# Issuing 24 DRAM stores of an FFT-and-FFN backward kernel from ScalarE's queue instead of SyncE's

## The chip, the cores and the metric

The kernel runs on one core of one Trainium2 chip. The metric is the device time of one execution in microseconds (us). Eleven executions of the kernel before had a median of 735.56 us (729.26 to 739.6). One further execution was profiled; it took 735.9 us, of which the profile covers a span of 734.2 us.

## The reference

The function computes a block with a gated state-space convolution and returns the output with the gradients of all parameters (outputs 0 to 11). Cut to what matters:

```python
xn = layernorm(x)                                     # x: 2048 x 512
K  = einsum(C, exp(dt*A*l), dt*B).real                # one filter of length 2048 for each of 512 channels
y  = irfft(rfft(pad(xn)) * rfft(pad(K)))[:L] + xn*Dskip
o  = silu(xn @ w1) @ w2                               # w1: 512 x 1792, w2: 1792 x 512
out = x + y * silu(o)
grads = vjp(out)(grad_out)    # d x, d A, d B, d C, d log_dt, d Dskip, d w1, d w2
```

## The kernel before

Everything is bf16 with sums in PSUM. The 512 channels are four blocks `b` of 128; the 2048 positions are 16 tiles of 128. The Fourier transforms are matmuls in two steps with a DMA transpose between them.

- **Forward, about 20 to 267 us.** `gen_tables` makes the exponentials of block `b` on VectorE and ScalarE and the filter out of them (matmuls L447 and L458), and stores it to `Kd` (L482, from ScalarE's queue). `gen_conv_x` transforms block `b` of `xn` with `dft_fwd` (matmuls L286, transposes L288, matmuls L297 and L298) and stores the spectrum `U` to `Ud` (L497). `gen_conv_fwd` transforms the filter, loads `U` back (L488), stores the filter's spectrum `KX` to `KXd` (L511), multiplies the two and transforms back (`dft_inv`, matmuls L310 and L319). These generators are woven block by block. `gen_ffn_fwd` (matmuls L541 and L558) is paced against them and fills TensorE.
- **Gates, about 265 to 305 us.** `gen_gate_rows` makes `do`, the gradient of `o`, and `ds`, the gradient of `y`, on ScalarE, VectorE and GpSimd.
- **Backward of the convolution, about 315 to 468 us.** `gen_conv_bwd` transforms `ds`, loads `Ud` and `KXd` (L488), multiplies, transforms back and stores `dKd` (L657, from ScalarE's queue) and `dUd` (L667). `gen_ffn_da` is paced against it: matmuls L886 into `ps_da`, VectorE's product L888, store `DHd` (L891), then for each 128 rows the matmuls L897 into `ps_dx`, ScalarE's copy of it to the tile `pd_s`, and the store of `pd_s` to `Pd` (L900). `pd_s` has one buffer, so that its next copy waits until the store has landed. `gen_out` makes output 0 (loads L614, L616, L618).
- **Gradients of the state-space parameters and of the weights, about 468 us to the end.** `gen_ssm_bwd` (loads L680 and L711, transposes L718, matmuls L729, L751 and L755), the rest of `gen_ffn_da` until 543 us, `gen_dw2` (L929), `gen_ln_bwd` (which loads `Pd` at L964), and last, from 671 us, `gen_dw1` (L947) alone on TensorE.

`k.evc` and `k.evb` are helpers of class `Evac` with the pattern "A": their copies out of PSUM run on ScalarE and all stand at L44 in the profile. So `U`, `KX` and `pd_s` are all written by ScalarE.

The order of the instructions on each engine isn't that of the source alone. The generators give priorities, and a scheduler orders the instructions when the program is built, with its own estimate of when each one could run; it inserts all waits too. Each engine then runs its list in order, and an instruction that waits holds all behind it on that engine. [...] SyncE computes nothing here: it issues DMAs, 24 of them the stores of this change.

Of the kernel before, what the change touches and what calls it, by code (L numbers as in the profile page):

```python
# [121 lines left out]
def turned_rows(k, pool, src, c, name, ev):  # L122

    out = pool.tile([P, 8, P], BF16, name=name, tag=name, bufs=2)
    turned(k, lambda i: src[:, 2 * c + i // 4, i % 4 * P:i % 4 * P + P], 8, out, ev)
    return out
# [149 lines left out]
def dft_fwd(k, w8, U, ev):  # L276

    nc, pc = k.nc, k.pc
    A = w8.tile([P, 2, 16, P], BF16, name="dA", tag="w8")
    Av = A[:].rearrange("p c g (t e) -> p c g t e", e=8)  # L280
    B = w8.tile([P, 2, 16, P], BF16, name="dB", tag="w8")
    for c in range(2):
        for h in range(2):
            ps = pc.tile([P, 8, P], F32, name="ps_s1", tag="pc")
            for j in range(8):
                nc.tensor.matmul(out=ps[:, j], lhsT=k.TF[:, 8 * h + j, c, :], rhs=U(8 * h + j), start=True, stop=True)  # L286
            ev(Av[:, c, :, 8 * h:8 * h + 8, :], ps[:].rearrange("p t (g e) -> p g t e", e=8))
        nc.sync.dma_start_transpose(B[:, c], A[:, c].rearrange("p g k -> p (g k)"))  # L288
    for _ in range(LAG):
        yield  # L290
    F2 = k.F2
    for h in range(2):
        for c, (m0, m1) in enumerate(((0, 1), (2, 0))):
            ps = pc.tile([P, 8, P], F32, name="ps_s2", tag="pc")
            for u in range(2):
                g0 = 8 * h + 4 * u
                nc.tensor.matmul(out=ps[:, 4 * u:4 * u + 4], lhsT=F2[:, m0], rhs=B[:, 0, g0:g0 + 4, :], start=True, stop=False)  # L297
                nc.tensor.matmul(out=ps[:, 4 * u:4 * u + 4], lhsT=F2[:, m1], rhs=B[:, 1, g0:g0 + 4, :], start=False, stop=True)  # L298
            ev(A[:, c, 8 * h:8 * h + 8, :], ps[:])
    return A, B  # L300


def dft_inv(k, A2, Y, ev, consume):

    nc, pc = k.nc, k.pc
    for g0 in range(0, 16, 4):
        ps = pc.tile([P, 4, 32, 8], F32, name="ps_i2", tag="pc")
        for g in range(4):
            for c in range(2):
                nc.tensor.matmul(out=ps[:, g], lhsT=Y[:, c, g0 + g, :], rhs=k.I2[:, c].rearrange("p c m -> p (c m)"),  # L310
                                 start=(c == 0), stop=(c == 1))
        ev(A2[:].rearrange("p c t (g e) -> p g (c t) e", e=8)[:, g0:g0 + 4], ps[:])
    yield
    for h in range(2):
        ps = pc.tile([P, 8, P], F32, name="ps_i1", tag="pc")
        for j in range(8):
            t = 8 * h + j
            for c in range(2):
                nc.tensor.matmul(out=ps[:, j], lhsT=k.TI[:, 2 * t + c, :], rhs=A2[:, c, t, :], start=(c == 0), stop=(c == 1))  # L319
        consume(8 * h, 8, ps)  # L320


def cplx_mul(k, w8, a, b, conj=False):

    TT = k.nc.vector.tensor_tensor
    n = 8
    for g0 in range(0, 16, n):
        gs = slice(g0, g0 + n)
        t2 = w8.tile([P, 2, n, P], BF16, name="cm2", tag="cm2")
        TT(out=t2[:, 0], in0=b[:, 1, gs], in1=a[:, 1, gs], op=ALU.mult)  # L330
        TT(out=t2[:, 1], in0=b[:, 0, gs], in1=a[:, 1, gs], op=ALU.mult)
        TT(out=b[:, :, gs], in0=b[:, :, gs], in1=a[:, 0:1, gs].to_broadcast([P, 2, n, P]), op=ALU.mult)  # L332
        TT(out=b[:, 0, gs], in0=b[:, 0, gs], in1=t2[:, 0], op=ALU.add if conj else ALU.subtract)  # L333
        if conj:
            TT(out=b[:, 1, gs], in0=t2[:, 1], in1=b[:, 1, gs], op=ALU.subtract)
        else:
            TT(out=b[:, 1, gs], in0=b[:, 1, gs], in1=t2[:, 1], op=ALU.add)
# [148 lines left out]
def spectrum_in(k, w8, b, which):  # L486
    t = w8.tile([P, 2, 16, P], BF16, name="sp_in", tag="w8")
    k.nc.sync.dma_start(t[:].rearrange("p c g k -> p (c g k)"), {"U": k.Ud, "K": k.KXd}[which][b])  # L488
    return t


def gen_conv_x(k, b):

    bs = slice(b * P, b * P + P)
    dft = k.dft
    U, _ = yield from dft_fwd(k, dft, lambda t: k.xn[:, t, bs], k.evc)
    k.nc.sync.dma_start(k.Ud[b], U[:].rearrange("p c g k -> p (c g k)"))  # L497
    yield


def gen_conv_fwd(k, b):

    nc, dft = k.nc, k.dft
    bs = slice(b * P, b * P + P)
    Kb = dft.tile([P, 4, 16, 32], BF16, name="Kb", tag="t4")
    nc.sync.dma_start(Kb[:].rearrange("p a t q -> p a (t q)"), k.Kd[b].rearrange("a i (r s) x -> (i r) a (s x)", s=2))
    for _ in range(LAG):
        yield
    KX, A2 = yield from dft_fwd(k, dft, lambda t: Kb[:, :, t, :], k.evc)
    U = spectrum_in(k, dft, b, "U")  # L510
    nc.sync.dma_start(k.KXd[b], KX[:].rearrange("p c g k -> p (c g k)"))  # L511
    yield
    cplx_mul(k, dft, KX, U)
    S = dft.tile([P, 16, P], BF16, name="S_b", tag="t4")

    def consume(t0, n, ps):
        xd = dft.tile([P, 8, P], BF16, name="xd", tag="cm2")
        nc.vector.tensor_tensor(out=xd[:], in0=k.xn[:, t0:t0 + n, bs], in1=k.Dbc[:, bs].unsqueeze(1).to_broadcast([P, n, P]), op=ALU.mult)
        nc.vector.tensor_tensor(out=S[:, t0:t0 + n], in0=ps[:], in1=xd[:], op=ALU.add)
    yield from dft_inv(k, A2, U, k.evc, consume)  # L520
    k.S_b = S
    (nc.scalar if b == 3 else nc.sync).dma_start(k.Sd[b], S[:].rearrange("p t d -> p (t d)"))
    yield
# [336 lines left out]
def gen_ffn_da(k, da):  # L860
    nc = k.nc
    D, FT, DK, T = k.D, k.FT, k.DK, k.T
    for c in range(T // 2):
        if c == 0:
            dN = turned_rows(k, da, k.do, 0, "doT", k.evb)
        dT = dN
        dTv = dT[:].rearrange("p (t k) n -> p t k n", k=DK)
        dhs = []
        for f in range(FT // 2):
            if f in (0, 4):  # L870
                n = 8 if f == 0 else 6
                sl = da.tile([P, 8, 256], BF16, name="slope", tag="slope", bufs=2)
                dh = da.tile([P, 8, 256], BF16, name="dhT", tag="dhT", bufs=3)
                nc.sync.dma_start(sl[:, 0:n], k.Hd[2 * f:2 * f + n, :, 256 * c:256 * c + 256].rearrange("f p n -> p f n"))
                nc.scalar.activation(out=dh[:, 0:n], in_=sl[:, 0:n], func=ACT.Silu)
                nc.scalar.activation(out=sl[:, 0:n], in_=sl[:, 0:n], func=ACT.Tanh, scale=0.5)
                slope_less_one(nc, dh[:, 0:n], sl[:, 0:n])
                dhs.append(dh)
            if f == 4 and c + 1 < T // 2:
                dN = turned_rows(k, da, k.do, c + 1, "doT", k.evb)  # L880
            i0 = 2 * (f % 4)
            ps = k.pf.tile([P, 2, 256], F32, name="ps_da", tag="pf")
            for j in range(2):
                ft = 2 * f + j
                for dk in range(DK):
                    nc.tensor.matmul(out=ps[:, j], lhsT=k.W2[:, ft, dk * P:dk * P + P], rhs=dTv[:, :, dk, :],  # L886
                                     start=(dk == 0), stop=(dk == DK - 1))
            nc.vector.scalar_tensor_tensor(out=dh[:, i0:i0 + 2, :], in0=dh[:, i0:i0 + 2, :], scalar=1.0, in1=ps[:], op0=ALU.add, op1=ALU.mult)  # L888
            if f in (3, 6):
                f0, n = (0, 8) if f == 3 else (8, 6)  # L890
                nc.sync.dma_start(k.DHd[f0:f0 + n, :, 256 * c:256 * c + 256].rearrange("f p n -> p f n"), dh[:, 0:n])  # L891
            yield
        for t in range(2):
            pd = da.tile([P, D], BF16, name="pd_s", tag="pd_s", bufs=1)
            ps = k.pf.tile([P, D], F32, name="ps_dx", tag="pf")
            for ft in range(FT):
                nc.tensor.matmul(out=ps[:], lhsT=dhs[ft // 8][:, ft % 8, t * P:t * P + P], rhs=k.W1[:, :, ft * P:ft * P + P],  # L897
                                 start=(ft == 0), stop=(ft == FT - 1))
            k.evb(pd[:], ps[:])
            nc.sync.dma_start(k.Pd[:, 2 * c + t, :], pd[:])  # L900
            yield


# [81 lines left out]
def kernel(ctx, tc, A_u, A_A_re, A_A_im, A_B_re, A_B_im, A_C_re, A_C_im, A_log_dt, A_Dskip, B_x, B_w1, B_w2, grad_out,  # L985
# [125 lines left out]
    for i in range(4):  # L1111
        next(bwd)
    ffb = gen_ffn_da(k, da)
    paced(bwd, woven([ffb, out], [2, 1]), BR)
    es_x.close()
# [35 lines left out]
```

## Time and profile before

| | |
|---|---|
| median of 11 executions | 735.56 us |
| profiled execution, and its span | 735.9 us, 734.2 us |
| mean granted TensorE clock | 0.934 of full speed |
| TensorE busy | 602.2 us, 5500 matmuls |
| VectorE busy | 548.2 us |
| ScalarE busy | 507.1 us |
| GpSimd busy | 108.1 us |
| SyncE's DMA queue q1 | 135.29 MB, packets 69.8% of 16 engines' span |
| ScalarE's DMA queue q10 | 4.98 MB, 2.1% |

In a line on a group or a wait, L12 is line 12 of the kernel; `out<-in` gives the tiles. PE is TensorE, ACT ScalarE, DVE VectorE, POOL GpSimd, SP SyncE; with a q behind it, the name means the engine's sequencer (issuing a DMA or handling a semaphore) and not its arithmetic. Issuing a DMA isn't counted as busy time. "us to landing" is the time from a DMA's issue until its last byte is confirmed.

### The profile page before, as it was taken

How to read it: one execution, taken by the hardware profiler on the slowest of the kernel's cores; microseconds unless marked ns; L12 is line 12 of the kernel's file. 1: busy time of each engine (PE TensorE's matmuls, PEld its weight loads, DVE VectorE, ACT ScalarE, POOL GpSimd, SP SyncE). 2: the span in 40 equal slices, each digit the busy share in tenths (PEclk: the TensorE clock that was granted, in tenths of full speed). 3: DMA queues.
4: the chain of work that ended last, by engine and by line, in shares of the span. 5: the costliest groups of instructions: out<-in, count | busy, mean ns of one | idle time of the engine just before them, and what ended most of it. 6: DMA issues, size and time to landing. Idle time of an engine off the chain costs nothing.

```text
span 734.2 us, 14020 instructions
## 1 busy us (share of the span) xinstructions
PE 602.2 (82%) x5500; PEld 432.1 (59%) x5500; DVE 548.2 (75%) x1086; ACT 507.1 (69%) x707; POOL 108.1 (15%) x180
## 2 busy tenths in 40 slices
PE   0668969979999966577989889978799978889995
PEld 0435646565675643354757567657576655656784
DVE  6969996969988759878898789747796685896000
ACT  6777758779889866947979688636746867782211
POOL 2172100000010035700000000000002003113210
PEclk9777998989999996879999989999999989999998
DMA  9876847769679876589988954789989999831772
GB/s 284 314 175 191 268 169 198 274 169 288 270 195 281 323 265 162 168 197 282 315 194 269 239 171 170 180 189 220 223 168 256 276 253 264 227 131 56 154 185 60
DMA packets 207042, 159.26 MB, mean 217 GB/s; under 512 B 129024, under 2 KB 185344, under 8 KB 203392
## 3 DMA queue, kind: packets, MB, share of 16 engines
q1 hardware_dynamic: 193856, 135.29, 69.8%
q0 software_dynamic: 6224, 18.10, 7.0%
q10 hardware_dynamic: 6896, 4.98, 2.1%
q8 instruction: 43, 0.70, 0.4%
q14 instruction: 23, 0.19, 0.1%
HBM read 65.14 MB, written 62.26 MB: 174 GB/s over the span
## 4 chain that ended last, share of the span: by engine, by line
issue 52%; POOL 5%; DVE 5%; DMA 3%; PE 0%; ACT 0%; POOLq 0%; ACTq 0%; SPq 0%; DVEq 0%
DMA out_dram<-o 1%; POOL out_dram L932 1%; DMA out_dram<-gout 1%; DVE YD L599 1%; DMA Kd<-KE 1%; POOL out_dram L809 1%; POOL out_dram L624 1%; DVE ds L595 1%; DMA Gr<-in_grad_out_dram 1%; DVE sp_in L332 1%; POOL out_dram L951 1%; POOL out_dram L980 1%; POOL g L598 0%; DVE YD L603 0%; DVE YD L601 0%
## 5 line engine op out<-in xcount | busy, mean ns | idle before, releaser
L44 ACT CAST dA<-ps_s 128x1024 bf16<-128x1024 f32 x96 | 94.2, 1031 | 18.7 <-PE ps_s L298 10.2
L886 PE MATMUL ps_da<-doT,W 128*128 128x256 bf16 x448 | 61.9, 281 | 9.8 <-DVE dhT L888 5.8
L541 PE MATMUL ps_h<-XT,W 128*128 128x256 bf16 x448 | 63.6, 293 | 1.3 <-ACT hT L44 0.7
L310 PE MATMUL ps_i<-I,sp_in 128*128 128x256 bf16 x384 | 53.5, 283 | 8.8 <-DVE sp_in L333 4.2
L558 PE MATMUL ps_o<-W,aT 128*128 128x512 bf16 x224 | 57.1, 393 | 2.8 <-ACT aT L549 2.6
L739 DVE TENSOR_TENSOR Tp<-Vb,Eb 128x1344 bf16<-128x1344 bf16 x64 | 51.9, 851 | 6.7 <-issue 5.4
L886 PEld LDWEIGHTS <-W 128*128 128x128 bf16 x448 | 44.2, 101 | 19.8 <-issue 11.4
L897 PE MATMUL ps_dx<-W,dhT 128*128 128x512 bf16 x224 | 54.7, 384 | 0.5 <-ACT doT L44 0.5
L44 ACT CAST dB<-ps_i 128x1024 bf16<-128x1024 f32 x48 | 47.0, 1019 | 10.6 <-PE ps_i L310 8.2
L541 PEld LDWEIGHTS <-W 128*128 128x128 bf16 x448 | 46.2, 105 | 13.1 <-issue 2.7
L947 PE MATMUL ps_w<-dh_tok,xn 128*128 128x256 bf16 x448 | 50.4, 273 | 2.2 <-DMA dh_tok<-DHd 1.7
L929 PE MATMUL ps_w<-YD,a_tok 128*128 128x512 bf16 x224 | 52.1, 379 | 0.0
L44 ACT CAST o<-ps_w 128x256 bf16<-128x256 f32 (+1 forms) x42 | 18.6, 443 | 48.3 <-PE ps_w L947 41.3
L310 PEld LDWEIGHTS <-sp_in 128*128 128x128 bf16 x384 | 37.1, 101 | 23.7 <-DVE sp_in L333 8.2
L947 PEld LDWEIGHTS <-xn 128*128 128x128 bf16 x448 | 43.4, 98 | 8.3 <-issue 3.1
L44 ACT CAST Vb<-ps_v 128x672 bf16<-128x672 f32 x64 | 43.0, 731 | 6.2 <-PE ps_v L729 6.2
L888 DVE SCALAR_TENSOR_TENSOR dhT<-dhT,ps_da 128x512 bf16<-128x512 bf16 x56 | 37.4, 682 | 12.9 <-PE ps_da L886 12.3
L729 PE MATMUL ps_v<-Gb,YT 128*128 128x168 bf16 x256 | 28.8, 243 | 18.4 <-ACT Vb L44 14.8
L297 PE MATMUL ps_s<-dB,F 128*128 128x512 bf16 x96 | 38.5, 407 | 5.9 <-DMA dB<-dA 4.1
L286 PEld LDWEIGHTS <-TF 128*128 128x128 bf16 x384 | 27.4, 105 | 25.3 <-issue 14.6
L419 ACT ACTIVATE sn<-V 128x1024 bf16<-128x1024 int32 (+3 forms) x40 | 34.8, 886 | 8.3 <-DVE V L417 8.1
L298 PE MATMUL ps_s<-dB,F 128*128 128x512 bf16 x96 | 38.0, 401 | 1.9 <-DMA dB<-dA 1.9
(223 smaller groups left out, 1384.0 us busy)
## 6 DMA issues: line engine op xcount, KB each, us to landing
Yd<-YD SPq DMA_DIRECT2D x8, 1024.0 KB, 5.4
sp_in<-Ud SPq DMA_DIRECT2D x8, 1024.0 KB, 7.4
h_in<-Hd SPq DMA_DIRECT2D x14, 512.0 KB, 5.4
Ed<-E SPq DMA_DIRECT2D x8, 672.0 KB, 5.4
Eb<-Ed SPq DMA_DIRECT2D x8, 672.0 KB, 5.6
Hd<-hT POOLq DMA_DIRECT2D x8, 512.0 KB, 6.5
Ud<-dA SPq DMA_DIRECT2D x4, 1024.0 KB, 9.6
KXd<-dA SPq DMA_DIRECT2D x4, 1024.0 KB, 6.3
```

Of the source, the lines that this page charges most:

```text
L44: return self.nc.scalar.copy(out=out, in_=in_)
L297: nc.tensor.matmul(out=ps[:, 4 * u:4 * u + 4], lhsT=F2[:, m0], rhs=B[:, 0, g0:g0 + 4, :], start=True, stop=False)
L298: nc.tensor.matmul(out=ps[:, 4 * u:4 * u + 4], lhsT=F2[:, m1], rhs=B[:, 1, g0:g0 + 4, :], start=False, stop=True)
L310: nc.tensor.matmul(out=ps[:, g], lhsT=Y[:, c, g0 + g, :], rhs=k.I2[:, c].rearrange("p c m -> p (c m)"), start=(c == 0), stop=(c == 1))
L541: nc.tensor.matmul(out=ps[:, j], lhsT=k.W1[:, dk, ft * P:ft * P + P], rhs=XTv[:, :, dk, :], start=(dk == 0), stop=(dk == DK - 1))
L558: nc.tensor.matmul(out=ps[:], lhsT=aT[:, ft, t * P:t * P + P], rhs=k.W2[:, ft, :], start=(ft == 0), stop=(ft == FT - 1))
L739: k.nc.vector.tensor_tensor(out=Tp[:, c, :, r ^ c].rearrange("p e (q w) a -> p q w e a", w=2), in0=Vb[:, :, c].rearrange("p q w (e a) -> p ...
L886: nc.tensor.matmul(out=ps[:, j], lhsT=k.W2[:, ft, dk * P:dk * P + P], rhs=dTv[:, :, dk, :], start=(dk == 0), stop=(dk == DK - 1))
L888: nc.vector.scalar_tensor_tensor(out=dh[:, i0:i0 + 2, :], in0=dh[:, i0:i0 + 2, :], scalar=1.0, in1=ps[:], op0=ALU.add, op1=ALU.mult)
L897: nc.tensor.matmul(out=ps[:], lhsT=dhs[ft // 8][:, ft % 8, t * P:t * P + P], rhs=k.W1[:, :, ft * P:ft * P + P], start=(ft == 0), stop=(ft ...
L929: nc.tensor.matmul(out=ps[:], lhsT=at[:, t, :], rhs=k.do[:, t, :], start=(t == 0), stop=(t == k.T - 1))
L947: nc.tensor.matmul(out=ps[:], lhsT=k.xn[:, t, dk * P:dk * P + P], rhs=dh[:, t].rearrange("p j n -> p (j n)"), start=(t == 0), stop=(t == k ...
```

## The change

Three stores are issued from ScalarE's queue and no longer from SyncE's. Four stores of `U`, four of `KX` (1 MB each) and sixteen of `pd_s` (128 KB each) are concerned. Nothing else in the source is changed; the scheduler orders the whole program anew.

```diff
@@ gen_conv_x
     U, _ = yield from dft_fwd(k, dft, lambda t: k.xn[:, t, bs], k.evc)
-    k.nc.sync.dma_start(k.Ud[b], U[:].rearrange("p c g k -> p (c g k)"))
+    k.nc.scalar.dma_start(k.Ud[b], U[:].rearrange("p c g k -> p (c g k)"))
@@ gen_conv_fwd
     U = spectrum_in(k, dft, b, "U")
-    nc.sync.dma_start(k.KXd[b], KX[:].rearrange("p c g k -> p (c g k)"))
+    nc.scalar.dma_start(k.KXd[b], KX[:].rearrange("p c g k -> p (c g k)"))
@@ gen_ffn_da
             k.evb(pd[:], ps[:])
-            nc.sync.dma_start(k.Pd[:, 2 * c + t, :], pd[:])
+            nc.scalar.dma_start(k.Pd[:, 2 * c + t, :], pd[:])
```

## The prediction

> **What bounds the kernel now.** I read the page's busy times first, then sums by stretch, then the waits of ScalarE and of SyncE's queue, and last single instructions in time.
>
> ```profile
> PE 602.2 (82%) x5500; PEld 432.1 (59%) x5500; DVE 548.2 (75%) x1086; ACT 507.1 (69%) x707; POOL 108.1 (15%) x180
> ```
>
> No engine is full. The stretches of 75 us (bounds; busy us and instructions of PE, PEld, DVE, ACT, POOL; granted clock; DMA share; GB/s) show who sets the pace where the sixteen Pd stores lie:
>
> ```profile
> 375.00:450.00 75.00, 65.15 (x550) 46.86 (x549) 64.04 (x92) 57.27 (x63) 4.04 (x6) 0.95 0.80 227
> 450.00:525.00 75.00, 64.09 (x623) 48.71 (x623) 53.59 (x73) 47.64 (x56) 0.51 (x1) 0.95 0.88 193
> ```
>
> TensorE is at 85 to 87%, ScalarE at 64 to 76%. So TensorE sets the pace, with 10 to 11 us idle in 75, and ScalarE has 17 to 27 us spare. A stall of ScalarE costs time only where TensorE then runs out of inputs or PSUM. TensorE's own waits, summed over its whole list, are 50.0 us for ScalarE (44 waits) and 56.8 us for VectorE (30 waits). I let half of a ScalarE stall reach the end.
>
> What SyncE's queue waits for (total us, times, longest):
>
> ```profile
> SPq L900 <- ACT pd_s L44: 17.9, 7, 4.2
> SPq L511 <- ACT dA L44: 12.5, 3, 6.0
> SPq L497 <- ACT dA L44: 1.5, 2, 0.9
> ```
>
> In 31.9 us SyncE stands at one of the 24 stores until ScalarE has copied, and all loads behind it stand too. That is what the change takes out of SyncE's list. Is anybody late because of it? ScalarE's waits for DMAs:
>
> ```profile
> ACT go_g L621 <- DMA go_g<-Od: 12.8, 6, 5.0
> ACT pd_s L44 <- DMA Pd<-pd_s: 3.6, 1, 3.6
> ACT dhT L875 <- DMA slope<-Hd: 3.3, 4, 1.3
> ```
>
> The longest of the first group ends at 421.11. SyncE before it:
>
> ```profile
> 407.08 7.16 SPq L288 DMA_TRANSPOSE dB<-dA  x2
> 414.34 0.57 SPq L891 DMA_DIRECT2D DHd<-dhT  x1
> 415.00 0.55 SPq L900 DMA_DIRECT2D Pd<-pd_s  x1
> 415.64 0.41 SPq L616 DMA_DIRECT2D go_g<-Od  x1
> ```
>
> The load of go_g was held by 7.16 us of issuing transposes and by 0.55 us of Pd. Most of those 12.8 us stay, then. The 3.6 us are another matter: that pd_s copy (489.99) waited for a Pd store whose data were ready at 471.2 and which SyncE, busy with transposes, issued only at 487.64. From ScalarE's queue it goes at once.
>
> [...] So I expect nothing of bandwidth. The trace agrees as far as it goes: 512 KB of Sd landed in 2.6 us from ScalarE and in 3.0 us from SyncE. [...] the trace shows ScalarE idle for 2.38 us while four Kd stores are issued. [...] Then a store from ScalarE could stand behind a transpose that SyncE is issuing. The only pair of this kind in the trace is at the start:
>
> ```profile
> 1.26 0.45 ACTq L1039 DMA_DIRECT2D Dbc<-in_A_Dskip_dram  x1
> 1.26 1.24 SPq L346 DMA_TRANSPOSE par_Ar<-in_A_A_re_dram  x1
> ```
>
> ScalarE wasn't held there, with queues still empty. No row shows it with full ones.
>
> **The change part by part**, against the profiled execution of 735.9 us (span 734.2 us, 1.7 us around it).
>
> (a) Issuing. Removed from SyncE are 24 issues at a median of 0.32 to 0.37 us, 8.5 us; SyncE isn't the limit, so this by itself gives nothing. Added to ScalarE are 24. The nearest rows are its own:
>
> ```profile
> 352.15 0.57 ACT L44 CAST pd_s<-ps_dx 128x512 bf16<-128x512 f32 x1
> 352.27 0.42 ACTq L657 DMA_DIRECT2D dKd<-dK  x1
> 352.74 1.93 ACT L44 CAST dB<-ps_i 128x1024 bf16<-128x1024 f32 x2
> ```
>
> The store of dK (copied until 352.25) is issued while the next copy runs, and the copy after that starts 0.02 us behind it: one instruction between copy and store hides the issue. Without it ScalarE loses 0.37 us and about 0.1 us of overlap between neighbours. In the changed program's order, 8 of the 24 stores stand directly behind their copy (one KX, seven Pd); 13 have one instruction between, 3 more. Sum: 8 x 0.47 = 3.8 us of ScalarE, half of it on the path: **+1.9**. If the cover of the 16 others were gone too: 24 x 0.47 = 11.3 us of ScalarE.
>
> (b) New waits. Fifteen of the 24 stores also wait for an earlier DMA [...]. Behind each stand ScalarE's copies out of PSUM, and TensorE behind those. The closest case is the tenth Pd store, which waits for the par_Br transpose only 83 instructions earlier in the program; that one is issued behind two transposes of 1.3 us, while ScalarE has a 1.5 us activation, the next pd_s copy and another 1.5 us before it. I bound all fifteen by 0 below and by three stalls of 3 us above and take one of 2 us, half on the path: **+1**.
>
> (c) [...] SyncE issues 24 dB transposes at a median of 3.3 us (80 us of the 381 between 54 and 435 us, 21%) and YT and par transposes in about half of 468 to 550 us (median 1.7 us). At half a transpose per hit: 17 stores x 0.21 x 1.65 = 5.9, and 7 x 0.5 x 0.85 = 3.0; together 8.9 us of ScalarE. Below, 0, by the pair at 1.26. I take a third, 3 us, half on the path: **+1.5**.
>
> (d) SyncE's list runs freer. Above: all of the 12.8, 3.6 and 3.3 us that ScalarE waits for go_g, Pd and slope, halved, about 10. Below: 0. I take the 3.6 us whole, of which half counts, and little else: **-2**. Next late would be the transposes themselves, which stay on SyncE.
>
> (e) The order. TensorE's list has the same 5500 matmuls, but moved: in the backward convolution those of L310, L319 and L297 stand 3 to 12 us of matmul time earlier, those of L886 up to 19 us later, some of L541 up to 28 us later; the last part (L947 alone) is as before. Counting in the program the waits of TensorE on ScalarE or VectorE whose producer stands under 10 instructions earlier, I find 63 where there were 55. At TensorE's mean wait for ScalarE, 50.0 / 44 = 1.1 us, eight more cost up to 9 us; the same moves could as well close gaps, so -4 below. I take **+2.5**.
>
> Sum: 1.9 + 1 + 1.5 - 2 + 2.5 = +4.9, so 740.8 us as a profiled execution. The median of the runs shown is 0.3 us under it: **740.5 us**.
>
> **Rivals.**
> - No measurable change, 736 us. Issues are hidden, and the reordering evens out. For it: ScalarE's 17 to 27 us spare per stretch, 16 of 24 stores not directly behind their copies (there the change isn't even what its words say). Chance 0.22.
> - Faster, 728 us. The relief of SyncE's list decides: loads and transposes come earlier by part of the 31.9 us, and (d) gives 8 with nothing given back. It decides if go_g's 12.8 us fall under 5 us and (a) to (c) stay under 2 us. Against it: the long holds on SyncE are its own transposes. Chance 0.18.
> - Much slower, 751 us. [...] 8.9 (c) + 3.8 (a) + 3 (b) reach TensorE whole, 15.7, while (d) and (e) about cancel; less the 0.3 to the median. It decides once ScalarE's stores take over 1 us each at the median. Chance 0.15.
> - The forecast, +0.7%, its own range 737 to 746. Chance 0.45, of which 0.05 lies under the bound below.
>
> **How the numbers follow.** A measurement of this kernel can tell about 0.5% (3.7 us) from no change. Faster is the third case's 0.18; same is 0.22 + 0.05 = 0.27; slower 0.40 + 0.15 = 0.55. The range reaches into the faster case by (d) with little given back, 730, and over the much slower one, 753.
>
> **What would show it.** (a): ScalarE's DMA issues at L497, L511 and L900 near 0.37 us each, and few gaps behind them. (b): ScalarE's waits naming a DMA ahead of these lines. (c): such an issue of over 1 us while SyncE has a transpose. (d): no wait of pd_s for Pd; go_g still waited for. (e): TensorE's busy time unchanged, its idle time moved between stretches, the sum some 5 us larger. I would be wrong if the waits of go_g vanish and the span falls, or if ScalarE's busy share stays and TensorE's idle time grows by over 10 us.

## The result and the profile after

The changed kernel took 747.2 us at the median of 12 executions (742.75 to 753.68). The kernel before took 735.64 us beside it (47 executions). The ratio is 1.0166, 95% interval 1.0142 to 1.0189. The change costs 1.7%, or 12 us; the forecast was 740.5 us. Disturbed executions are left out of all comparisons. The profiled executions have spans of 744.8 and 734.2 us, both at a mean clock of 0.934.

The page of the changed kernel, busy times and DMA queues:

```profile
PE 603.7 (81%) x5500; PEld 432.8 (58%) x5500; DVE 548.9 (74%) x1086; ACT 507.3 (68%) x707; POOL 102.0 (14%) x180
...
q1 hardware_dynamic: 190400, 124.80, 63.7%
...
q10 hardware_dynamic: 10352, 15.47, 5.8%
```

The work is the same: no engine's busy time grows by more than 1.5 us, and GpSimd's falls by 6. The bytes of the 24 stores have moved from q1 to q10. So the time lies in waits. TensorE's waits, summed over its whole list, are 130.0 us where they were 120.4.

What the stores cost where they now stand. First all sixteen of Pd (duration in ns: minimum, median, maximum; then from issue to landing), then one store on ScalarE's list, then a store of the spectrum `U` and the transpose that SyncE was issuing at the time:

```profile
L900 ACTq DMA_DIRECT2D Pd<-pd_s x16: 326/327/457, 357.4 to 557.0; - x16
...
DMA to landing us min/median/max: 1.7/3.3/6.0
```

```profile
64.35 0.62 ACT L44 CAST hT<-ps_h 128x512 bf16<-128x512 f32 x1
64.51 0.34 ACTq L497 DMA_DIRECT2D Ud<-dA  x1
65.00 1.91 ACT L549 ACTIVATE aT<-hT 128x2048 bf16<-128x2048 bf16 x1
...
235.41 0.33 ACTq L497 DMA_DIRECT2D Ud<-dA  x1
```

```profile
230.12 5.68 SPq L288 DMA_TRANSPOSE dB<-dA  x1
```

A store took 0.33 us of the sequencer. The copy of hT ends at 64.97 and aT starts at 65.00, so this issue cost nothing. The store at 235.41 is issued in its usual 0.33 us while SyncE is still issuing a transpose (230.12 to 235.80), though only in the last 0.4 us of it; the first experiment below has one further inside. The longest of the 24 stores took 0.457 us.

Two waits of ScalarE that the prediction named, and the longest wait of SyncE's queue that has to do with the tables:

```profile
ACT go_g L621 <- DMA go_g<-Od: 7.5, 6, 2.1
...
ACT pd_s L44 <- DMA Pd<-pd_s: 1.7, 4, 0.8
```

```profile
SPq L435 <- DVE YD L434: 36.3, 5, 12.8
```

SyncE waits at no store of this change any more (31.9 us before). It waits longer at a store that stays, that of the tables' `Y` (36.3 us, 21.4 before). That wait isn't the loss by itself: the first experiment below, which isn't slower, has 32.7 us of it.

The stretches that the prediction started from:

```profile
375.00:450.00 75.00, 65.62 (x578) 47.09 (x577) 64.86 (x94) 62.35 (x66) 4.36 (x7) 1.00 0.82 234
450.00:525.00 75.00, 64.50 (x595) 48.11 (x596) 52.36 (x72) 43.97 (x51) 0.51 (x1) 0.95 0.78 191
```

TensorE is no less busy here than before. The place to look is earlier. The first matmul L886 opens the backward part. Its line (durations in ns, first and last start) in the kernel before:

```profile
L886 PE MATMUL ps_da<-doT,W x448: 269/273/422, 318.9 to 537.1; 128*128 128x256 bf16 x150
```

and in the changed kernel:

```profile
L886 PE MATMUL ps_da<-doT,W x448: 269/273/421, 329.4 to 550.1; 128*128 128x256 bf16 x150
```

It starts 10.5 us later. The span is 10.6 us longer. In this pair of profiles all of the loss has come about before any Pd store is issued (the first at 357.4). Only the eight stores of spectra stand ahead of it.

One place in the changed kernel shows how, between 235 and 249 us. TensorE first, then ScalarE, then VectorE; what stands in brackets is the idle time ahead of the instruction and who ended it:

```profile
237.88 0.38 PE L297 MATMUL ps_s<-dB,F 128*128 128x512 bf16 x1
241.16 0.59 PE L298 MATMUL ps_s<-dB,F 128*128 128x512 bf16 x1 [2.90 <-DMA dB<-dA]
241.54 0.63 PE L297 MATMUL ps_s<-dB,F 128*128 128x512 bf16 x1
241.96 0.63 PE L298 MATMUL ps_s<-dB,F 128*128 128x512 bf16 x1
...
244.10 2.90 PE L558 MATMUL ps_o<-W,aT 128*128 128x512 bf16 x12
```

```profile
239.35 0.95 ACT L419 ACTIVATE sn<-V 128x896 bf16<-128x896 int32 x1
245.74 0.58 ACT L44 CAST ob<-ps_o 128x512 bf16<-128x512 f32 x1 [5.43 <-PE ps_o L558]
246.22 1.02 ACT L44 CAST dA<-ps_s 128x1024 bf16<-128x1024 f32 x1
247.12 0.61 ACT L44 CAST ob<-ps_o 128x512 bf16<-128x512 f32 x1
247.60 0.55 ACT L419 ACTIVATE sn<-V 128x384 bf16<-128x384 int32 x1
```

```profile
241.80 1.34 DVE L442 TENSOR_TENSOR W<-E,CT 128x672 bf16<-128x672 bf16 x3
248.18 0.43 DVE L422 TENSOR_TENSOR H<-sn,mag 128x192 bf16<-128x192 bf16 x2 [5.04 <-ACT sn L419]
```

TensorE's list has a transform of block 3 ahead of twelve matmuls L558; its data are not there, and it waits. ScalarE's list has the copy of L558's result ahead of the last sine of the tables, so the sine waits too: its own input was ready at about 241.9 (L417 on VectorE), and it starts at 247.60. VectorE waits for the sine before it can make `H`. So VectorE waits for ScalarE, ScalarE for TensorE and TensorE for the transpose: a chain that only the order of the lists makes. In the kernel before, the same instructions on the same three engines:

```profile
230.16 4.05 PE L558 MATMUL ps_o<-W,aT 128*128 128x512 bf16 x18
234.05 2.78 PE L541 MATMUL ps_h<-XT,W 128*128 128x256 bf16 x24
236.67 0.38 PE L297 MATMUL ps_s<-dB,F 128*128 128x512 bf16 x1
```

```profile
234.25 0.58 ACT L44 CAST ob<-ps_o 128x512 bf16<-128x512 f32 x1
...
235.94 0.52 ACT L419 ACTIVATE sn<-V 128x384 bf16<-128x384 int32 x1 [0.24 <-DVE V L417]
```

```profile
235.77 1.33 DVE L442 TENSOR_TENSOR W<-E,CT 128x672 bf16<-128x672 bf16 x3
237.02 0.41 DVE L422 TENSOR_TENSOR H<-sn,mag 128x192 bf16<-128x192 bf16 x2
```

There L558 and L541 run while the transpose is under way, and the sine waits only 0.24 us. `H` comes 11.2 us earlier (237.02 for 248.18). The three `W` in front of it come 6.0 us earlier (235.77 for 241.80), so about 5 us of this arise here and the rest further up.

The delay is then handed on. On SyncE's list the load of the filter (`Kb`, L506) and behind it the load of `Gr` (L576) are issued at 274.83 and 275.30 (263.69 and 264.11 before), and VectorE begins the gates with `Gr`, changed kernel first, then the kernel before:

```profile
281.02 3.15 DVE L595 TENSOR_TENSOR ds<-Gr,g 128x1024 bf16<-128x1024 bf16 x3 [6.91 <-DMA Gr<-in_grad_out_dram]
```

```profile
269.33 2.73 DVE L595 TENSOR_TENSOR ds<-Gr,g 128x1024 bf16<-128x1024 bf16 x3 [7.07 <-DMA Gr<-in_grad_out_dram]
```

That is 11.7 us later. So the 10.5 us at the first L886 are there at `H` already (11.2 us).

### The profile page after: what moved, and what is told of

It is laid out like the page before. It is cut to its first block, busy times and chain, and to the rows that moved or that the text cites. A ratio compares the mean times of both kernels' runs of the same rounds, so it can differ in the third digit from the quotient of the medians.

```text
span 744.8 us, 13992 instructions
## 1 busy us (share of the span) xinstructions
PE 603.7 (81%) x5500; PEld 432.8 (58%) x5500; DVE 548.9 (74%) x1086; ACT 507.3 (68%) x707; POOL 102.0 (14%) x180
## 4 chain that ended last, share of the span: by engine, by line
issue 29%; DVE 21%; PE 17%; ACT 13%; DMA 11%; POOL 4%; SPq 3%; ACTq 1%; POOLq 0%; DVEq 0%
ACT dA L44 3%; PE ps_o L558 3%; PE ps_dx L897 2%; PE ps_i L310 2%; DVE W L442 2%; PE ps_da L886 2%; ACT sn L419 2%; DMA dB<-dA 1%; ACT dB L44 1%; PE ps_v L729 1%; PE ps_h L541 1%; DVE sp_in L332 1%; DMA Pd<-pd_s 1%; SPq L346 1%; DVE V L414 1%
## 5 line engine op out<-in xcount | busy, mean ns | idle before, releaser
L310 PE MATMUL ps_i<-I,sp_in 128*128 128x256 bf16 x384 | 56.6, 292 | 20.7 <-DVE sp_in L333 16.9
L541 PE MATMUL ps_h<-XT,W 128*128 128x256 bf16 x448 | 63.2, 294 | 5.2 <-ACT ob L44 3.9
L886 PE MATMUL ps_da<-doT,W 128*128 128x256 bf16 x448 | 61.0, 280 | 7.5 <-DVE dhT L888 4.0
L558 PE MATMUL ps_o<-W,aT 128*128 128x512 bf16 x224 | 56.6, 396 | 4.4 <-ACT aT L549 3.5
L541 PEld LDWEIGHTS <-W 128*128 128x128 bf16 x448 | 46.2, 105 | 17.4 <-issue 6.8
L886 PEld LDWEIGHTS <-W 128*128 128x128 bf16 x448 | 44.1, 100 | 17.3 <-issue 9.3
L297 PE MATMUL ps_s<-dB,F 128*128 128x512 bf16 x96 | 39.2, 415 | 7.5 <-DMA dB<-dA 3.6
L298 PE MATMUL ps_s<-dB,F 128*128 128x512 bf16 x96 | 39.0, 412 | 5.5 <-DMA dB<-dA 5.5
```

The source lines that it names most:

```text
L541: nc.tensor.matmul(out=ps[:, j], lhsT=k.W1[:, dk, ft * P:ft * P + P], rhs=XTv[:, :, dk, :], start=(dk == 0), stop=(dk == DK - 1))
L558: nc.tensor.matmul(out=ps[:], lhsT=aT[:, ft, t * P:t * P + P], rhs=k.W2[:, ft, :], start=(ft == 0), stop=(ft == FT - 1))
```

## The experiments

Theory: the stores themselves cost nothing, and the new order of the instructions on all engines makes the loss. Rivals: the stores' place makes it (on ScalarE, or missing on SyncE); or only one half of the stores does; or one engine's list does.

To hold an order, each instruction of an engine is tied to the one ahead of it, with no semaphore, so that the scheduler has no choice; stores are left out of the chain where their place is to be free:

```diff
+for a, b in zip(names, names[1:]):     # names: one engine's list, in the wanted order
+    tc.add_manual_dep(here[b], a, DependencyInfo(NoSync, DATA), reason="fixed order")
```

All ratios are to the kernel before on the same chip, with 95% intervals. "First L886" and "rest" (from there to the end of the span, both in us) come from each run's one profile; the mean clocks of these profiles lie between 0.920 and 0.943. Read a time off the ratio, and only the place of a loss off the last two columns.

| run | stores on ScalarE | order, forward / rest | ratio | first L886 | rest |
|---|---|---|---|---|---|
| before | none | old / old | 1 | 318.9 | 415.3 |
| the change | 24 | new / new | 1.0166 (1.0142 to 1.0189) | 329.4 | 415.4 |
| e1 | 24 | old / old | 0.9976 (0.9954 to 0.9998) | 317.9 | 415.6 |
| e2 | none | new / new | 1.0360 (1.0325 to 1.0396) | 328.3 | 437.1 |
| e3 | 16 Pd | the scheduler's own | 1.0053 (1.0031 to 1.0074) | 318.8 | 421.7 |
| e4 | 8 spectra | the scheduler's own | 1.0096 (1.0064 to 1.0127) | 330.7 | 411.9 |
| e5 | 24 | old / new | 1.0045 (1.0021 to 1.0068) | 316.7 | 420.5 |
| e6 | 24 | new / old | 1.0152 (1.0114 to 1.0189) | 334.2 | 411.1 |
| e7 | 24 | new, one sine moved / new | 1.0132 (1.0089 to 1.0175) | 322.4 | 419.4 |
| e8 | 24 | new, twelve L558 moved / new | 1.0175 (1.0140 to 1.0209) | 326.4 | 422.8 |
| e9 | 24 | new / new, again | 1.0204 (1.0157 to 1.0251) | 331.2 | 424.6 |
| e10 | 24 | new, SyncE old / new | 1.0343 (1.0292 to 1.0394) | 341.2 | 419.6 |
| e11 | 24 | new, VectorE old and sine / new | 1.0419 (1.0371 to 1.0466) | 346.6 | 419.1 |
| e12 | 24 | old, SyncE and GpSimd new / new | 1.0157 (1.0114 to 1.0200) | 326.8 | 418.4 |
| e13 | 24 | new, one sine moved / old | 1.0109 (1.0074 to 1.0144) | 328.1 | 417.0 |
| e14 | 8 spectra | old / old | 1.0002 (0.9970 to 1.0034) | 320.1 | 411.1 |
| e15 | 16 Pd | old / old | 0.9965 (0.9944 to 0.9986) | 318.5 | 419.5 |

**The stores moved, the old order kept (e1).** The changed kernel's three lines, and the chain above with the order of the kernel before.

> All 24 stores issued from ScalarE as in the changed kernel, but every other instruction of every engine held in the order of the kernel before. Order theory (the loss of about 11.6 us lies in the new order of the forward part, and a store on ScalarE's queue costs next to nothing): 733 to 738 us, first matmul of L886 near 319 us. Queue theory (the stores hold ScalarE's copies and the time is lost there): 743 us or more.

736.68 us, beside 738.7 before. First L886 in its profile:

```profile
L886 PE MATMUL ps_da<-doT,W x448: 269/273/422, 317.9 to 537.3; 128*128 128x256 bf16 x150
```

The 1.7% are gone, and what stays is 0.2% on the other side. So the order makes the loss. Between e1 and the changed kernel, which differ in the order alone (and in the waits that the scheduler derives from it), lies 1.0166 / 0.9976 = 1.0190, or 14 us.

A store of e1, and what SyncE was issuing at the time:

```profile
411.67 0.33 ACTq L900 DMA_DIRECT2D Pd<-pd_s  x1
```

```profile
409.31 4.98 SPq L288 DMA_TRANSPOSE dB<-dA  x1
```

The store begins 2.36 us into the transpose's issue, ends 2.29 us ahead of its end, and takes no longer than others.

**The order changed, the stores not moved (e2).** The kernel before, its stores on SyncE (left to be placed), all else chained in the changed kernel's order.

> The stores stay on SyncE, but every other instruction of every engine stands in the order of the changed kernel. Order theory: 744 to 750 us, first matmul of L886 near 329 us. Queue theory: 734 to 739 us.

766.1 us, far more than expected. The forward part loses as in the changed kernel (328.3), which the order theory foretold; it did not foretell the other 22 us behind it. ScalarE's waits show most of them:

```profile
ACT pd_s L44 <- DMA Pd<-pd_s: 22.1, 5, 17.2
```

In the new order on SyncE, the Pd stores come too late for the next copy into the single buffer `pd_s`: once ScalarE stood for 17.2 us, and TensorE for 10.0 us behind it. On ScalarE's queue the same wait is 1.7 us in all. So the new order needs the Pd stores on ScalarE's queue, and behind the forward part e2 tells nothing about the order alone.

**One half of the stores alone, with the scheduler's own order (e3, e4).**

```diff
 e3, gen_ffn_da only
-            nc.sync.dma_start(k.Pd[:, 2 * c + t, :], pd[:])
+            nc.scalar.dma_start(k.Pd[:, 2 * c + t, :], pd[:])
 e4, gen_conv_x and gen_conv_fwd only
-    k.nc.sync.dma_start(k.Ud[b], ...)
+    k.nc.scalar.dma_start(k.Ud[b], ...)
-    nc.sync.dma_start(k.KXd[b], ...)
+    nc.scalar.dma_start(k.KXd[b], ...)
```

> Only the sixteen Pd stores are moved; the scheduler leaves TensorE's list of the forward part as it was. Order theory: the forward part takes as long as before (first matmul of L886 near 319 us), and the total is within 733 to 739 us. Queue theory: 16 of 24 stores, about two thirds of the loss, 743 us.

> Only the four U and four KX stores are moved; TensorE's list is that of the changed kernel up to the end of the forward part. Order theory: the whole loss, 744 to 750 us, first matmul of L886 near 329 us. Queue theory: 8 of 24 stores, a third of the loss, 739 us.

741.91 and 743.76 us. In the forward part the scheduler gave e4 the changed kernel's lists, instruction for instruction, and e3 those of the kernel before. So the eight stores of spectra bring the late forward part (330.7), and Pd does not (318.8); but Pd costs 0.5% behind it, which was above what I expected and near the number of the queue theory. e15 below decides between the two.

**The two halves of the order apart (e5, e6).** Instructions up to the last one of the forward generators in one order, the rest in the other.

> The changed kernel; on each engine the instructions of the forward part, up to the last one of the forward generators, stand in the order of the kernel before, the rest in the changed kernel's own order; all 24 stores on ScalarE's queue. Order theory, with the whole loss in the forward part: the first L886 matmul comes near 318 us instead of 329 and the span is 744.8 - 10.5 = 734, so 733 to 737 us as a median and 0.997 to 1.003 of before. If the rest's order (which places the sixteen stores of Pd) costs by itself, as it did with the stores of Pd moved alone (+0.5%), 738 to 741 us.

> The other half: the changed kernel with its own order in the forward part (the eight stores of spectra left to be placed by the scheduler) and the order of the kernel before in the rest. Order theory, with the whole loss in the forward part: first L886 near 328 to 330 us, span 744 to 746, 1.012 to 1.019 of before. If the loss comes from the rest: 735 to 738 us.

742.07 and 748.97 us, beside 738.94 before. To the kernel before, the forward part's order costs 1.5% and the rest's order 0.45%. To e1, which has its stores in the same place, they cost 1.8% (plus or minus 0.4%) and 0.7% (plus or minus 0.3%), together more than the 1.9% of both at once, so they don't simply add up; and e4, with the new forward lists and Pd on SyncE, lies at 1.0096 only. The forward part is the larger share, but its size seems to depend on what stands behind it.

That the rest costs too was a rival's number in e5's expectation. I had read from the one profile of the changed kernel that the rest loses nothing (415.4 to 415.3). The table corrects this: the eight profiles with the rest in the new order and the stores on ScalarE have a median rest of 419.5 us, and the six with the old one (before, e1, e6, e13, e14, e15) have 415.5. The difference is 4.0 us, or 0.5%. The changed kernel's profile has the quickest rest of the eight, though its execution (746.6 us) was near the median of its kind. e9 has the same lists, instruction for instruction, and its rest took 9.2 us more at the same clock; its profiled execution was the slowest of six, and TensorE's waits come to 140.0 us in it, where they were 130.0.

> The changed kernel again, with each engine's list held as it is; timed beside the next three kernels so that they can be set against it. 1.014 to 1.019 of before, the first L886 matmul near 329 us.

e9's ratio, 1.0204, lies above its expectation, but its interval holds the 1.0166 of the changed kernel. So tying the instructions to one another doesn't make a program faster by itself.

The first L886 is steadier than the rest. With the old forward order it came at 316.7 to 320.1 us (six profiles), with the new one unedited at 328.3 to 334.2 (five, e4 among them).

**Which place in the forward part (e7, e8, e13).** e7 moves one instruction of ScalarE's list, e8 twelve of TensorE's, both in the place between 235 and 249 us. e13 is e6 with the sine of e7 moved.

```diff
 e7, e13: ScalarE
 L419 sn 128x896
+L419 sn 128x384
 L44  ob
 L44  dA
 L44  ob
-L419 sn 128x384
 e8: TensorE
 L541 ps_h x8
+L558 ps_o x12
 L297, L298 ps_s x8
-L558 ps_o x12
```

> The changed kernel in its own order, except that on ScalarE the last sine of the tables of block 3 (L419, 128x384, at 247.60 us) stands ahead of the copy of ob that waited 5.43 us for TensorE, two places up. If ScalarE's list by itself holds VectorE's wait of 5.04 us on the way to the filter sums: 5 us less, 741 to 743 us. If TensorE's list is the limit there (its matmuls from 241 to 252 us stay where they are, and only its waits of 0.68, 0.53 and 1.47 us behind them can close): 1 to 3 us less, 744 to 746 us.

> The changed kernel in its own order, except that on TensorE the twelve matmuls L558 that started at 244.10 us stand ahead of the matmuls L297 and L298 of block 3 that waited 2.90 us for a transpose at 241.16. If that place is one of those that make the loss: the 2.90 us of waiting go, ScalarE's copy of ob and the sine behind it come 3.5 to 4 us earlier, and the span is 3 to 6 us shorter, 741 to 744 us. If other waits take its place (the transposed data are then waited for further on): less than 1 us, 746 to 748.

> The changed kernel with its own order in the forward part and the old order in the rest (1.0152 without more), and in it the last sine of block 3 two places up in ScalarE's list, ahead of the copy of ob. If that sine holds 7 us, as the profile of the run with it alone showed (first L886 at 322.4 instead of 329.4): first L886 at 322 to 327 and 1.004 to 1.008 of before. If those 7 us were chance: 1.012 to 1.018.

In e7 the sine, `H` and the matmuls of the filter sums:

```profile
241.54 0.52 ACT L419 ACTIVATE sn<-V 128x384 bf16<-128x384 int32 x1 [1.68 <-DVE V L417]
241.97 0.57 ACT L44 CAST ob<-ps_o 128x512 bf16<-128x512 f32 x1
```

```profile
242.62 0.42 DVE L422 TENSOR_TENSOR H<-sn,mag 128x192 bf16<-128x192 bf16 x2
```

```profile
238.31 0.38 PE L298 MATMUL ps_s<-dB,F 128*128 128x512 bf16 x1 [0.50 <-DMA dB<-dA]
...
249.68 0.73 PE L447 MATMUL ps_k<-W,YD 128*128 128x84 bf16 x15
```

The waits of 5.43 and 5.04 us are gone, `H` comes 5.6 us earlier and these L447 come 5.0 us earlier than in the changed kernel (254.71). But TensorE's own wait was only 0.50 us here, and 2.90 in the changed kernel; one sine behind it can't have made that, so part of the 7.0 us in the first L886 is the chance of when the transpose landed, and this profile is of the quickest execution of e7. The medians say less: 1.0132 for 1.0166, and 1.0109 for 1.0152 (e13 for e6). Neither difference stands outside its interval alone; together they are 0.39%, plus or minus 0.36%, near 3 us. So e13 falls between its two expectations, and this place holds about a quarter of the forward loss. e8 took TensorE's wait down to 1.19 us and brought `H` forward to 245.00 and the first L886 to 326.4, but the time (1.0175) did not fall. It came out as the second of its expectations; which waits took the place of this one I have not followed.

**One engine's list put back (e10, e11, e12).** The forward part of one or more lists from the kernel before, the others from the changed one.

> The changed kernel; only SyncE's list of the forward part stands in the order of the kernel before, all other engines in the changed kernel's order. If the order of the computing engines makes the loss: as the changed kernel, 1.013 to 1.019 of before, first L886 at 328 to 331. If SyncE's order makes it (a store of the tables that waits for VectorE, with transposes behind it): first L886 back at 318 to 322, 1.003 to 1.008.

> The changed kernel; VectorE's list of the forward part in the order of the kernel before, and the last sine of block 3 ahead of the copy of ob, as in the run with the sine alone; TensorE, SyncE and the rest of ScalarE in the changed kernel's order. If the tables' own chain (VectorE and that sine) holds the loss: first L886 at 318 to 321, 7 us below the changed kernel, 1.004 to 1.008 of before. If TensorE's order holds what the sine didn't give back (about 3.5 us of 10.5): first L886 at 322 to 325, 1.010 to 1.014.

> The changed kernel; TensorE's, VectorE's and ScalarE's lists of the forward part in the order of the kernel before, SyncE's and GpSimd's in the changed kernel's order. If the computing engines' order makes the loss: as with the whole forward part in the old order, first L886 at 316 to 320, 1.002 to 1.007 of before. If SyncE's order matters too, it comes out between: first L886 at 321 to 327, 1.008 to 1.014.

762.96, 768.66 and 748.84 us, beside 737.12 before. Both theories miss in e10 and e11: one list put back makes it worse than all new. e12 misses by its ratio (1.0157; its first L886, 326.8, is within the second expectation). It shows a wait that arises where old and new lists meet. Its three computing engines are in the old order, SyncE's list is the new one:

```profile
165.81 1.25 PE L286 MATMUL ps_s<-Kb,TF 128*128 128x128 bf16 x10 [10.63 <-DMA Kb<-Kd]
```

```profile
134.44 0.34 SPq L435 DMA_DIRECT2D Yd<-YD  x1
157.60 0.32 SPq L424 DMA_DIRECT2D Ed<-E  x1
157.97 0.42 SPq L522 DMA_DIRECT2D Sd<-S_b  x1
158.57 0.77 SPq L506 DMA_DIRECT2D Kb<-Kd  x1
```

SyncE issued nothing from 134.78 to 157.60, when the store of `Ed` had waited 22.7 us for VectorE, and the load of `Kb` stands behind it in SyncE's new list. That suits the new lists of the others (TensorE waits for `Kb` 2.4 us in all in the changed kernel) and not the old ones. So the lists have to fit together: neither SyncE's nor VectorE's new list is slow by itself. TensorE's and ScalarE's were not put back alone, and the waits of e10 and e11 I have not followed.

**Each half of the stores in the old order (e14, e15).** As e3 and e4, with the chain.

> Only the eight stores of spectra on ScalarE's queue, every other instruction in the order of the kernel before. Order theory: 0.995 to 1.003 of before. If moved stores cost on ScalarE by themselves and the Pd stores gained it back: 1.004 or more.

> Only the sixteen stores of Pd on ScalarE's queue, every other instruction in the order of the kernel before. Order theory: 0.995 to 1.003 of before, and so 0.3 to 0.8% under the same move with the scheduler's own order (1.0053). If the 0.5% of that run is the price of issuing on ScalarE: 1.004 to 1.007.

739.58 and 736.05 us, beside 738.21. The spectra give nothing, Pd gains 0.35%. Against e3 (1.0053), which has the same stores on the same queues, e15 is 0.9% faster by its order. It has the lowest ratio of all runs, 0.35% under the kernel before and 2.0% under the changed one (1.0166 / 0.9965); e1's 0.9976 lies within its interval.

## Why the prediction was wrong

The sign was right: slower. The size was 4.9 us, and the median rose by 11.6. Step by step:

- **(a) Issuing, +1.9.** The durations were right (0.33 us at the median, expected near 0.37). That they reach the path was not: e1 has all 24 on ScalarE and is not slower. ScalarE's sequencer issued a store while the copy ahead still ran: the store from 64.51 to 64.85 above, the copy until 64.97.
- **(b) New waits, +1.** Fifteen semaphore instructions stand at these lines in the profile of the changed kernel (2 at L497, 2 at L511, 11 at L900; 17 ns each). The only idle time of ScalarE there that a DMA ended is the 1.7 us of `pd_s` for its own buffer, and e1 leaves no room for more. About 0.
- **(c) Stores held by SyncE's transposes, +1.5.** Refuted for these stores: 0.33 us well inside a transpose's 4.98 (e1), and no store above 0.457. That a store waits for half of a transpose's issue was my estimate, and no trace had shown it.
- **(d) SyncE relieved, -2.** Near in size, but not by its mechanism. With (a) to (c) near 0, e1's -0.24% (-1.8 us, barely clear of noise) and e15's -0.35% (-2.6 us) are left for this step by elimination. But the wait on which I built it, 3.6 us before, did not go in the old order, first in e1, then in e15:

```profile
ACT pd_s L44 <- DMA Pd<-pd_s: 4.8, 2, 3.0
```

```profile
ACT pd_s L44 <- DMA Pd<-pd_s: 4.6, 1, 4.6
```

So that the size is near is luck, and what gains these 2 us is not shown. In the old order go_g's wait stays (10.5 us in e1, 13.1 in e15, 12.8 before), as argued; in the changed kernel it fell to 7.5 us, and the kernel was no faster for it.

- **(e) The order, +2.5 with +9 as the bound.** This is the step that failed, by its size: 14 us between e1 and the changed kernel (1.9%, plus or minus 0.3%). The count was fair: TensorE's waits for ScalarE and VectorE rose from 74 to 86, where I had counted 8 more close pairs. The price was wrong. I took the mean wait of 1.1 us for each, as if each pair lost its own microsecond. Where the loss could be followed, one late instruction in a list held a chain on several engines, the sine for 5 us, and the delay then shows far behind as one long wait:

```profile
PE ps_i L310 <- DVE sp_in L333: 16.9, 9, 9.3
```

This was 4.2 us, 2 times, longest 3.4 before. The 9.3 us end at 307.17, when VectorE reaches `sp_in` among the products of the gates that began 11.7 us late; they look like the earlier delay arriving at TensorE, and not like a second loss. Where I looked was wrong too: I compared orders in the backward part, where the Pd stores lie, and the larger part (1.5% in e6) came from the forward part, which the eight stores of spectra reorder. The bound should have come from the chain that the tables of the last block form from sine to filter: TensorE has little other work behind it (28.5 of 53 us busy from 267 to 320 us before), so what is late at `H` (11.2 us) is late at the first L886 (10.5 us).

The rival "much slower" came nearest in time, 751 us, by a mechanism that is refuted: no store waited for a transpose. "Faster" asked for 8 us with go_g's waits nearly gone; moving the stores alone gave 1.8 us (e1) to 2.6 us (e15), with those waits still there.

What stays open: which other places make up the forward loss beside the sine, where the 0.5% of the rest arise, and what gains the 0.2 to 0.35% in the old order. SyncE's or VectorE's list put back alone doesn't tell, since it makes new waits.

## What to carry to other kernels

Where a scheduler orders the program, moving a DMA to another queue changes every engine's list, and the lists can be worth several times the DMA: here -0.2% for the move and +1.9% for the order. Test such a change with the old order held, and keep the two effects apart. In pricing a new order, don't count close pairs; find the dependent chain that has nothing beside it, and look for an instruction of it that stands in a list behind one which waits for another engine. Here one such instruction held about a quarter of the forward loss; the others were not found.

## What the runs showed of the hardware

- A store took 0.33 us of ScalarE's sequencer at the median (0.326 to 0.457 in the changed kernel), and the same 0.33 us when it began 2.36 us into a transpose that SyncE took 4.98 us to issue (e1).
- After its wait of 2.90 us TensorE ran the next seven matmuls of 512 columns at starts about 0.43 us apart (241.54, 241.96), where they were 0.22 apart at the same place in the kernel before (237.10 and 237.32). The granted clock was 0.50 of full speed from 241.00 to 244.20, and 1.00 from 236.00 to 238.40 in the kernel before. At this place they stand 0.43 apart in e6 and e9 too (waits of 3.51 and 3.63 us), and 0.22 apart in e7 and e8 (0.50 and 1.19 us). The length of a wait alone doesn't decide it: in the changed kernel the clock was 0.52 behind a wait of 2.38 us (from 70.26 to 71.50) and 1.00 behind one of 2.41 us (from 337.90 to 339.50). As an estimate from this one place, the lower clock behind the 2.90 us cost about 1.4 us on top: seven starts took 2.94 us (241.16 to 244.10) where 7 x 0.22 = 1.54 would do.
- Two profiles of one program, with the same lists and nearly the same clock (0.934 and 0.935), had spans of 744.8 and 755.8 us; TensorE's waits differ by 10.0 of these 11.0 us (130.0 and 140.0). A single span can't carry a difference of 1% here.
